# Linear attention with a GEGLU block on one core: the order of the k-v products and of v, and the size of the last q groups

One core of one Trainium2 chip. The metric is the device time of one execution in microseconds, taken on the slowest core, here the only one. All executions quoted are fast, at a granted TensorE clock of 1.0 (0.999 in some).

## The reference

A layer norm, an attention whose features are softmaxes of a small per-head product, a second layer norm and a GEGLU block, over 2048 rows of 640 columns, in bfloat16:

```python
pq = einsum("bhsd,hdf->bhsf", q, w_phi);  pk = einsum("bhsd,hdf->bhsf", k, w_phi)
phi_q = concat([softmax(pq), softmax(-pq)], -1);  phi_k = the same of pk
kv = einsum("bhsf,bhsd->bhfd", phi_k, v);  z = phi_k summed over s
o = einsum("bhqf,bhfd->bhqd", phi_q, kv) / (einsum("bhqf,bhf->bhq", phi_q, z)[..., None] + 1e-6)
h  = x + o.reshape(B, S, D) @ wo
h2 = h + (gelu(LN(h) @ w_gate) * (LN(h) @ w_up)) @ w_down
```

## The kernel before

The 2048 rows are 16 tiles of 128. For each tile t a loop issues the k projection (with `w_phi` folded in) and its two exponentials, then the v projection of tile t+4, the layer norm of tile t+6, whose transpose goes through a DMA to `LN1T`, and the normalising factors of k. At odd tiles the k-v products of two earlier tiles are added to an accumulator in PSUM. The order is set by hand, and in the traces PE's products come in the order in which they are written. In the profiles `pk` and `pv` are the k and v products of a tile, `wa` the folding of `w_phi` into the weights of q, `kvp` the k-v products, `pq` the products of a group of q and `Eq` their exponentials, `ab` and `po` the attention and output products of a tile, `gu` the gate and up products, `g` the gelu and `GT` its product with up. Shortened, with cuts marked:

```python
QG = ((0, 1), (2, 3), ..., (13, 14), (15,), (16, 17), (18, 19))   # groups of chunks of q

def kv_tile(t):                       # 20 products of 64 x 84, into one PSUM tile
    ...
for t in range(NT):
    ...
    k_tile(t)                         # 10 products, then two exponentials on ScalarE
    if t in FQ: fold(WqT, Wq2, ...)   # tiles 4 to 8: 6 small products ("wa")
    ...
    if t + 4 < NT: v_mm(t + 4)        # 10 products; they need tile t+4 of LN1T
    if t > 0 and t + 6 < NT: ln_ap(t + 6, on_act=True)   # layer norm, then the DMA transpose
    if t + 4 < NT: v_ev(t + 4)        # ScalarE copies v out of PSUM
    ...
    k_norm(t)
    if t % 2 == 1 and t >= 5:         # k-v products behind v
        kv_tile(t - 5)
        kv_tile(t - 4)

def q_mm(j):                          # one PSUM tile of two banks for a group
    pqs[j] = gtile("pq")
    for i, bc in enumerate(QG[j]): ...  # 5 products of 512 columns for each chunk
def q_exp(j, signs=(0, 1)):           # exp(x) and exp(-x) of the whole group
    for s in signs:
        nc.scalar.activation(Eq[j][:, :, s, :], pqs[j][:, 0:len(QG[j])], ACTF.Exp, scale=(1.0, -1.0)[s])
```

The loop has three PSUM tiles for k, v and the folded weights. Behind the loop the attention of the first tiles and the rest of q are interleaved on four PSUM tiles, and the gate and up products (`gu`) follow. A chunk of q is 128 features over 512 rows. Between the last exponential and the first gelu ScalarE loads another table (1.28 us in the trace).

The softmax here doesn't subtract the row's maximum and nothing guards it: scores larger than these inputs give would overflow.

## Time and profile before

| | before |
|---|---|
| time, median of 3 (later 6) | 280.98 (280.89) us |
| span of the profiled execution | 278.9 us |
| TensorE (PE) busy | 272.0 us |
| PE waits that the change is about | v of tile 9, v of tile 11, third gate/up group |

The change goes for three waits of PE. They are read in the timeline from start to start, since the ends that the profile gives for PE are modelled and overlap the next start. The groups of ScalarE by form, with the count, busy time and mean ns of one, price the exponentials of q:

```profile
L352 ACT ACTIVATE Eq<-pq 128x1024 bf16<-128x1024 f32 x18 | 17.5, 1026 | 3.7 <-PE pq L347 3.7
L352 ACT ACTIVATE Eq<-pq 128x512 bf16<-128x512 f32 x4 | 2.2, 612 | 0.0
```

One instruction over two chunks (1026 ns) is cheaper than two over one each (2 x 612 ns). The other lines of this profile stand in the prediction; its list of PE's waits shows three of six rows, and the three left out (0.2 to 0.4 us) lie in the first 16 us.

### The profile page before, as it was taken

The page shows a single profiled execution, that of the slowest core. Times are in us where ns is not written, and L with a number is a line of the kernel's source. Part 1 is how long each engine was busy: PE and PEld are TensorE (multiplying, and loading weights), DVE is VectorE, ACT ScalarE, POOL GpSimd, SP SyncE. Part 2 cuts the span into 40 slices and gives each one's busy share as a digit, 9 for nine tenths or more (in the row PEclk, how much of TensorE's full clock was granted, in tenths as well). Part 3 has the DMA queues.
Part 4 walks back from the last instruction along what each step waited for, and adds up shares of the span by engine and source line. Part 5 has one row for each costly group of instructions (what it writes and reads, how often), then busy time and mean ns, then how long its engine had stood idle before and what let it go on. Part 6 is the DMA issues. An engine that isn't in the chain of part 4 may idle for free.

```text
span 278.9 us, 5775 instructions
## 1 busy us (share of the span) xinstructions
PE 272.0 (98%) x2322; PEld 171.8 (62%) x2337; DVE 165.0 (59%) x289; ACT 142.3 (51%) x235; POOL 95.8 (34%) x211
## 2 busy tenths in 40 slices
PE   7999999999999999999999999999999999999995
PEld 2677677764655788788864555675455567444574
DVE  5799997789396586576324848322667532333222
ACT  4669988768596847355524354413446340222200
POOL 3448997685202216455401243300135230000000
DMA  7995222893440021314120113221041413000011
GB/s 208 271 244 83 51 51 47 175 396 138 144 143 0 2 48 26 71 46 98 27 71 2 40 21 61 44 75 47 2 47 24 74 24 94 26 1 0 0 49 47
DMA packets 40635, 21.05 MB, mean 75 GB/s; under 512 B 33440, under 2 KB 38816, under 8 KB 40608
## 3 DMA queue, kind: packets, MB, share of 16 engines
q1 hardware_dynamic: 40608, 20.68, 29.9%
q8 instruction: 18, 0.29, 0.5%
q14 instruction: 9, 0.07, 0.1%
HBM read 10.18 MB, written 2.62 MB: 46 GB/s over the span
## 4 chain that ended last, share of the span: by engine, by line
PE 89%; DMA 3%; ACT 2%; DVE 2%; issue 1%; POOL 1%; SPq 0%
PE gu L588 37%; PE pd L609 19%; PE pq L347 8%; PE po L543 8%; PE pk L260 7%; PE pv L260 5%; PE ab L483 3%; PE kvp L325 2%; DMA LN1T<-ln 2%; DMA x_sb<-in_A_x_dram 1%; ACT Eq L352 1%; DVE stats L108 1%; ACT sq L357 1%; PE wa L224 1%; PE tp L145 1%
## 5 line engine op out<-in xcount | busy, mean ns | idle before, releaser
L594 DVE TENSOR_TENSOR GT<-gu,g 128x512 bf16<-128x512 f32 (+1 forms) x60 | 34.4, 580 | 55.2 <-ACT g L591 55.1
L591 ACT ACTIVATE g<-gu 128x512 bf16<-128x512 f32 (+1 forms) x60 | 30.7, 512 | 69.1 <-PE gu L588 68.2
L588 PE MATMUL gu<-LN2T,Wg 128*128 128x512 bf16 (+1 forms) x289 | 61.3, 335 | 1.0 <-DVE GT L594 0.4
L588 PE MATMUL gu<-LN2T,Wu 128*128 128x512 bf16 (+1 forms) x300 | 61.8, 336 | 0.0
L609 PE MATMUL pd<-Wd,GT 128*128 128x320 bf16 (+2 forms) x396 | 53.8, 295 | 0.0
L609 PEld LDWEIGHTS <-GT 128*128 128x128 bf16 x396 | 38.0, 98 | 15.3 <-DVE GT L594 0.9
L588 PEld LDWEIGHTS <-Wu 128*128 128x128 bf16 x300 | 29.3, 98 | 22.6
L588 PEld LDWEIGHTS <-Wg 128*128 128x128 bf16 x300 | 28.3, 98 | 21.3 <-issue 0.5
L260 PEld LDWEIGHTS <-LN1T 128*128 128x128 bf16 x290 | 27.6, 98 | 11.6 <-DMA LN1T<-ln 0.7
L307 POOL TENSOR_TENSOR vt<-vS,rs 128x672 bf16<-128x672 bf16 x22 | 29.7, 1371 | 8.7 <-DVE rs L303 7.0
L614 DVE TENSOR_TENSOR y<-pd,x_sb 128x640 bf16<-128x640 f32 (+3 forms) x18 | 13.5, 750 | 30.2 <-PE pd L609 30.2
L491 ACT COPY AB<-ab 128x704 f32<-128x704 f32 x28 | 19.6, 748 | 19.8 <-PE ab L483 19.6
L299 DVE TENSOR_REDUCE sk<-E 128x64 f32<-128x1280 bf16 x16 | 23.1, 1446 | 3.7 <-ACT E L292 3.7
L292 ACT ACTIVATE E<-pk 128x640 bf16<-128x640 f32 x32 | 20.9, 707 | 7.9 <-PE pk L260 7.7
L524 DVE TENSOR_TENSOR tt<-AB,w 128x1280 bf16<-128x1280 f32 x16 | 23.8, 1486 | 1.1 <-POOL w L517 0.9
L543 PE MATMUL po<-Wo,oT 128*128 128x320 bf16 x160 | 24.4, 299 | 0.0
L260 PE MATMUL pk<-Wk,LN1T 128*128 128x320 bf16 x160 | 24.2, 299 | 0.0
L347 PE MATMUL pq<-LN1T,Wq 128*128 128x512 bf16 x96 | 22.7, 379 | 0.2
L352 ACT ACTIVATE Eq<-pq 128x1024 bf16<-128x1024 f32 (+1 forms) x22 | 19.4, 951 | 3.7 <-PE pq L347 3.7
L260 PE MATMUL pv<-Wv,LN1T 128*128 128x320 bf16 x130 | 20.0, 299 | 0.5 <-DMA LN1T<-ln 0.5
L543 PEld LDWEIGHTS <-oT 128*128 128x128 bf16 x160 | 15.5, 98 | 7.3 <-DMA oT<-o 0.5
L132 ACT ACTIVATE ln<-x_sb,v,rstd 128x640 bf16<-128x640 bf16 x14 | 12.9, 919 | 11.3 <-POOL v L571 11.1
(89 smaller groups left out, 262.9 us busy)
## 6 DMA issues: line engine op xcount, KB each, us to landing
out_dram<-y SPq DMA_DIRECT2D x15, 160.0 KB, 1.8
Wg<-in_B_w_gate_dram SPq DMA_DIRECT2D x1, 1920.0 KB, 8.5
Wu<-in_B_w_up_dram SPq DMA_DIRECT2D x1, 1920.0 KB, 15.0
Wd<-in_B_w_down_dram SPq DMA_DIRECT2D x1, 1920.0 KB, 8.0
x_sb<-in_A_x_dram SPq DMA_DIRECT2D x2, 640.0 KB, 5.5
Wo<-in_A_wo_dram SPq DMA_DIRECT2D x1, 800.0 KB, 9.5
x_sb<-in_A_x_dram SPq DMA_DIRECT2D x4, 160.0 KB, 3.1
Wv<-in_A_wqkv_dram SPq DMA_DIRECT2D x2, 320.0 KB, 4.4
```

The source lines that it names most:

```text
L260: nc.tensor.matmul(ps[:, u, 0:HD], lhsT=lnT(t, c), rhs=W[:, c, u * HD:(u + 1) * HD], start=(c == 0), stop=(c == NC - 1))
L292: nc.scalar.activation(Ek[t][:, s, :].rearrange("p (u f) -> p u f", u=2), pk[:, :, 0:HD], ACTF.Exp, scale=(1.0 if s == 0 else -1.0))
L299: nc.vector.reduce_sum(sk, Ek[t].rearrange("p s (h f) -> p (s h) f", f=Dh), axis=AX.X)
L307: eng.tensor_tensor(vt[:, s], vS[t % 8], rs[:, s * H:(s + 1) * H, None].to_broadcast([P, H, VC]), ALU.mult)
L347: nc.tensor.matmul(pqs[j][:, i, :], lhsT=Wq2[:, kc, c * P:(c + 1) * P], rhs=LN1T[b][:, kc, :], start=(kc == 0), stop=(kc == NC - 1))
L352: nc.scalar.activation(Eq[j][:, :, s, :], pqs[j][:, 0:len(QG[j])], ACTF.Exp, scale=(1.0, -1.0)[s])
L524: nc.vector.tensor_tensor(tt.rearrange("p s (h f) -> p s h f", f=Dh), num, w[:, :, :, None].to_broadcast([P, 2, H, Dh]), ALU.mult)
L543: nc.tensor.matmul(po[:, u, 0:HD], lhsT=st[t][:, c, :], rhs=Wo[:, c, u * HD:(u + 1) * HD], start=(c == 0), stop=(c == NC - 1))
L588: nc.tensor.matmul(gu[:, i, 0:n], lhsT=W[:, c, f * P:(f + 1) * P], rhs=LN2T[b][:, c, a0:a1], start=(c == 0), stop=(c == NC - 1))
L591: nc.scalar.activation(g[:, 0:n], gu[:, 0, 0:n], ACTF.Gelu_apprx_tanh)
L594: nc.vector.tensor_tensor(st[b, "g", f][:, a0:a1], gu[:, 1, 0:n], g[:, 0:n], ALU.mult)
L609: nc.tensor.matmul(pd[:, u, n0:n1], lhsT=st[b, "g", f][:, tl * P:(tl + 1) * P], rhs=Wd[:, f, u * HD + n0:u * HD + n1], start=(f == 0), sto ...
```

## The change

Two independent parts. The k-v products of a pair of tiles go ahead of the next v, so that PE has work while v waits. And the last four chunks of q, two groups of two before, become four groups with their own PSUM tiles and exponentials, so that ScalarE is done sooner after the last product of q and can change its table.

```diff
-    QG = (..., (15,), (16, 17), (18, 19))
+    QG = (..., (15,), (16,), (17,), (18,), (19,))
...
+        if t % 2 == 1 and t >= 5:
+            kv_tile(t - 5)
+            kv_tile(t - 4)
         if t + 4 < NT:
             v_mm(t + 4)
...
         k_norm(t)
-        if t % 2 == 1 and t >= 5:
-            kv_tile(t - 5)
-            kv_tile(t - 4)
...
     attn_c(1)
-    q_mm(q + 5)
-    q_exp(q + 5)
+    for j in (q + 5, q + 6):
+        q_mm(j)
+        q_exp(j)
     attn_ln(0, True); attn_d(1, False); attn_e(0, True, True)   # (three lines, unchanged)
-    q_mm(q + 6)
-    q_exp(q + 6)
+    for j in (q + 7, q + 8):
+        q_mm(j)
+        q_exp(j)
```

More of the change, by code (lines that the diff above doesn't have):

```diff
@@ L50 @@
     FQ = (4, 5, 6, 7, 8)
-    QG = ((0, 1), (2, 3), (4, 5), (6,), (7, 8), (9, 10), (11, 12), (13, 14), (15,), (16, 17), (18, 19))
+    QG = ((0, 1), (2, 3), (4, 5), (6,), (7, 8), (9, 10), (11, 12), (13, 14), (15,), (16,), (17,), (18,), (19,))
     QT = (15, 15, 15, 15)
@@ L682 @@
     attn_a(2, 2)
-    assert q + 7 == len(Eq)
+    assert q + 9 == len(Eq)
     def attn_at(t, i, offs):
```

## The prediction

> **What bounds the kernel now.** I read the page first. TensorE (PE) is busy 272.0 us of a 278.9 us span and carries 89% of the chain that ended last.
>
> ```profile
> span 278.9 us, 5775 instructions
> PE 272.0 (98%) x2322; PEld 171.8 (62%) x2337; DVE 165.0 (59%) x289; ACT 142.3 (51%) x235; POOL 95.8 (34%) x211
> ```
>
> So whatever is to be won lies in at most 278.9 - 272.0 = 6.9 us of PE idle time. Of that, 1.24 us stands before the first matmul and most of the rest in the first 16 us and in the store at the end, which the change does not touch. Next I read the waits of PE alone. Its columns are engine, line, what was waited for, us in total, times and the longest.
>
> ```profile
> PE wu L206 <- DVE zero L191: 1.2, 1, 1.2
> PE pv L260 <- DMA LN1T<-ln: 0.5, 1, 0.5
> PE gu L588 <- DVE GT L594: 0.4, 1, 0.4
> ```
>
> The second and third rows are the two places where the change acts: one wait of a v product for its transposed input, and one wait of the first gate/up products for a PSUM buffer. To price them I read the timeline of PE around each (start, duration, line, operation, count, idle time before it).
>
> ```profile
> 30.46 1.52 PE L260 MATMUL pk<-Wk,LN1T 128*128 128x320 bf16 x10
> 31.82 0.48 PE L224 MATMUL wa<-BD,WqT 128*128 128x140 bf16 x6
> 32.77 1.53 PE L260 MATMUL pv<-Wv,LN1T 128*128 128x320 bf16 x10 [0.48 <-DMA LN1T<-ln]
> 34.23 0.95 PE L325 MATMUL kvp<-vt,E 128*64 128x84 bf16 x40
> 35.12 1.53 PE L260 MATMUL pk<-Wk,LN1T 128*128 128x320 bf16 x10
> ...
> 39.52 0.48 PE L224 MATMUL wa<-BD,WqT 128*128 128x140 bf16 x6
> 40.02 1.52 PE L260 MATMUL pv<-Wv,LN1T 128*128 128x320 bf16 x10
> 41.47 0.96 PE L325 MATMUL kvp<-vt,E 128*64 128x84 bf16 x40
> 42.36 0.85 PE L260 MATMUL pk<-Wk,LN1T 128*128 128x320 bf16 x5
> ```
>
> Durations overlap, because ends are modelled; I therefore work with the distance between starts. Six wa products take 29.10 - 28.79 = 0.31 us where nothing holds them up, so PE was free at 31.82 + 0.31 = 32.13 and really lost 32.77 - 32.13 = 0.64 us, not 0.48. By the same measure pv at 40.02 came 40.02 - 39.83 = 0.19 us late. No DMA is named there. In the order of instructions this pv reuses the PSUM buffer that the previous v leaves, and ScalarE (ACT) copied that one out from 39.27 to 39.97.
>
> The second place, ACT, PE and VectorE (DVE) side by side:
>
> ```profile
> 91.24 1.94 ACT L352 ACTIVATE Eq<-pq 128x1024 bf16<-128x1024 f32 x2 [0.50 <-PE pq L347]
> 93.20 1.28 ACT L591 ACT_TABLE_LOAD   x1
> 94.49 0.38 ACT L591 ACTIVATE g<-gu 128x256 bf16<-128x256 f32 x1
> ...
> 94.91 0.42 DVE L594 TENSOR_TENSOR GT<-gu,g 128x256 bf16<-128x256 f32 x1 [1.20 <-ACT g L591]
> ...
> 94.30 0.71 PE L588 MATMUL gu<-LN2T,Wu 128*128 128x256 bf16 x5
> 95.39 0.71 PE L588 MATMUL gu<-LN2T,Wg 128*128 128x256 bf16 x5 [0.37 <-DVE GT L594]
> ```
>
> It is one chain: last exponentials of q, table load, first gelu, its product, and only then is the buffer of the first gate/up group free for the third group. Five products of 256 columns take 0.55 us from start to start (94.30 - 93.76), so PE was free at 94.85 and lost 0.54 us.
>
> **What the Trainium skill says.** "TensorE: Matmul & The Clock Gate", section Back-to-back issue gap, gives N/2.4 + 2.5 ns for a warm matmul, 136 ns at 320 columns; here ten take 1.36 us (30.46 to 31.82), so PE runs at that rate and moving products makes none cheaper. The same page, Step-by-step: what each phase is for, says that matmuls stay in program order and only weight loads are pulled ahead; the trace agrees, as ready k-v products stood behind the waiting v at 32.77. "ScalarE: Activation LUTs", section What ACT_TABLE_LOAD costs, gives 186 ns + 0.833 ns per element for an activation with immediate scale and bias, 93 ns of overlap, and about 1283 ns for a load. The trace has 612 and 1026 ns for 512 and 1024 columns and 1283 ns for the load, which agrees; the page's extra 1380 ns of drain is not seen, the gelu starts 0.01 us after the load. "Perfetto Trace Analysis", section Optimizing Scalar/DVE Operations, advises breaking up instructions of an unsaturated engine that causes bubbles on others; the second half of the change does that.
>
> **The change, part 1: k-v products ahead of v.** The count of PE instructions stays 2322. At tiles 5, 7, 9 and 11 forty k-v products (0.89 us, 34.23 to 35.12) change places with the ten v products. Are they ready? The first pair needs products that POOL and DVE had finished by 29.2 us, so yes, by 3 us. At tile 5 PE then runs: wa ends 32.13, about 0.10 us for the switch to 64-column products (v before k-v takes 1.46 instead of 1.36 us today, so this is paid either way), k-v to 33.12, v to 34.48. Its input landed by about 32.7, so it no longer waits. The next k starts at 34.48 instead of 35.12: **0.64 us**. At tile 7 everything is 0.64 earlier. The v-copy on ACT that held the buffer follows its own v and ends near 39.33; PE reaches the k-v products at 39.2 and v only at 40.18. So the 0.19 is hidden too: k at 41.54 instead of 42.36, **0.82 us** in all. At tiles 9 and 11 v starts without a delay today (46.76, 53.19), so the swap brings nothing. Its cost is that each v is copied out 0.89 us later relative to the k before it; ACT has 1.24, 0.78 and 0.88 us of idle time before the exponentials of the following k, and that is the gap it eats.
>
> **Part 2: single groups.** Four activations of 1024 columns become eight of 512. ACT pays 4 x (0.48 + 0.61) - 2 x (0.92 + 1.02) = 0.48 us more (spacing and last duration of each form), inside 1.94 and 0.50 us that it idles there. The path gets shorter: chunk 18 is done before chunk 19 ends, so from 91.24 only two short exponentials are left, 0.48 + 0.61 = 1.09 us instead of 1.94. Table load from 92.35, gelu at 93.64, its product about 94.05 to 94.47, which is before PE asks at 94.85. The wait goes: **0.54 us**.
>
> **Sum**: 0.82 + 0.54 = 1.36 us of span. I take off 0.1 for small new waits: 281.0 - 1.3 = **279.7 us**.
>
> **Rivals.** (1) The input wait moves on instead of going. One transpose took 4.3 us to land where most take 2.6; v of tile 10 would now want its input at 36.16 instead of 36.80, and if that transfer (issued 31.71) takes 4.3 it lands at 36.0. For it: the margin is 0.15 us. Against: at 36.80 no wait is seen. It would leave about 0.2 + 0.54: 280.2 us. (2) PSUM takes the place. A single group occupies a whole one of four buffers and half of it is empty, so the second half of the attention product of tile 2 now waits for chunk 18's exponentials, done at about 91.24, and is wanted at 91.42. If ACT runs 0.3 us late there, PE waits and part 2 brings 0.2 or less: 280.1 us. (3) The gain of part 2 is given back at 101.48, where the output product of tile 2 takes its weights just as a DMA transpose lands (the trace shows 0.16 us of waiting). PE comes there 0.54 us earlier; only if DVE also gets earlier is nothing lost. For DVE: its work for that tile stands behind the first two gelu products, which move 0.4 to 0.9 us forward, so the transpose should land at about 100.6, before 100.97. If not, 280.2 us. (4) Nothing at all, if the 4.3 us landing is an accident of the profiled execution and the untimed ones never wait: then only part 2 counts, 280.4 us.
>
> **Range and chances.** All rivals lie between 279.7 and 281, and nothing in the change can touch the 98% that PE works. The three runs before differ by 1.4 us, more than the gain, so I give 278.8 to 280.9. Two per cent is 5.6 us, nearly the whole idle time of PE, so faster by that much gets 0.02. Slower would take a new wait of 5 us or a slow execution: 0.01.
>
> **What would show it.** Right: PE's waits no longer name LN1T for pv and GT for gu; the k after the first k-v products starts near 34.5 and the one after the second near 41.5; the table load starts near 91.5 (93.20 less 0.82 from part 1 and 0.85 from part 2); PE busy time stays 272. Wrong: a new wait of pv for LN1T or ACT between 36 and 42, a wait of ab for Eq near 90.6, or a wait for oT near 100; or a span that falls by less than 0.8 us.

## The result, and the profile after

| | before | after |
|---|---|---|
| time, median of 6 (range) | 280.89 us (280.68 to 282.08) | 279.53 us (279.02 to 280.40) |
| ratio, 95% interval | | 0.9947 (0.9922 to 0.9972) |
| span of the profiled execution | 278.9 us | 278.0 us |
| PE busy | 272.0 us | 272.2 us |

A ratio is the mean time of one kernel's fast runs over that of the other's of the same rounds, so it is not quite the ratio of the medians. The interval leaves 1 out. The medians differ by 1.36 us, which the prediction had as its sum before it took 0.1 off. The profiled spans differ by only 0.9 us, and that needs an explanation. The waits of PE after:

```profile
PE wu L206 <- DVE zero L191: 1.2, 1, 1.2
PE pv L260 <- DMA LN1T<-ln: 0.3, 1, 0.3
PE wa L224 <- DVE Wk L235: 0.2, 1, 0.2
PE pv L276 <- DVE LN1T L146: 0.2, 1, 0.2
```

The wait for GT is gone. A wait of pv for LN1T is still in the list, but the timeline of PE shows that it is a different one:

```profile
23.83 1.53 PE L260 MATMUL pv<-Wv,LN1T 128*128 128x320 bf16 x10 [0.31 <-DMA LN1T<-ln]
...
30.95 1.52 PE L260 MATMUL pk<-Wk,LN1T 128*128 128x320 bf16 x10
32.31 0.48 PE L224 MATMUL wa<-BD,WqT 128*128 128x140 bf16 x6
32.72 0.95 PE L325 MATMUL kvp<-vt,E 128*64 128x84 bf16 x40
33.60 1.53 PE L260 MATMUL pv<-Wv,LN1T 128*128 128x320 bf16 x10
34.97 1.52 PE L260 MATMUL pk<-Wk,LN1T 128*128 128x320 bf16 x10
...
39.36 0.48 PE L224 MATMUL wa<-BD,WqT 128*128 128x140 bf16 x6
39.77 0.96 PE L325 MATMUL kvp<-vt,E 128*64 128x84 bf16 x40
40.66 1.53 PE L260 MATMUL pv<-Wv,LN1T 128*128 128x320 bf16 x10
42.03 1.52 PE L260 MATMUL pk<-Wk,LN1T 128*128 128x320 bf16 x10
```

The first row is v of tile 6, which started at 23.35 in before and now waited, long before anything that the change moves; PE is 0.49 us late from there (k of tile 5 at 30.95 instead of 30.46). The k after the first k-v products then stands at 34.97 instead of 35.12: against k of tile 5 it is 0.64 us earlier. The next one, at 42.03 instead of 42.36, is 0.82 us earlier by the same measure. ScalarE and PE around the change of table:

```profile
87.38 2.16 ACT L352 ACTIVATE Eq<-pq 128x512 bf16<-128x512 f32 x4 [0.86 <-PE pq L347]
89.81 2.17 ACT L352 ACTIVATE Eq<-pq 128x512 bf16<-128x512 f32 x4 [0.27 <-PE pq L347]
92.00 1.28 ACT L591 ACT_TABLE_LOAD   x1
93.29 0.38 ACT L591 ACTIVATE g<-gu 128x256 bf16<-128x256 f32 x1
```

```profile
93.96 0.71 PE L588 MATMUL gu<-LN2T,Wu 128*128 128x256 bf16 x5
94.50 0.71 PE L588 MATMUL gu<-LN2T,Wg 128*128 128x256 bf16 x5
```

The table load came 1.31 us after the start of the last transposes (90.69), before 2.16 us (91.04 to 93.20): 0.85 us earlier. The third gate/up group follows the second without a gap, 0.54 us after 93.96, where before there were 1.09.

To compare runs in spite of accidents in the start-up I use three stretches of PE's timeline, from start to start: from k of tile 0 to k of tile 5 (start-up), from there to k of tile 12 (where part 1 acts), and from there to the third gate/up group (where part 2 acts). In us:

| | start-up | part 1's stretch | part 2's stretch |
|---|---|---|---|
| before | 14.36 | 25.07 | 39.86 |
| after | 14.85 | 24.25 | 39.30 |
| change | +0.49 | -0.82 | -0.56 |

The three add up to -0.89, the 0.9 us between the spans. What lies outside them is the same in these two (16.10 us ahead of k of tile 0; 183.51 and 183.50 from the third gate/up group to the end), but over all fourteen profiles it varies: 15.89 to 16.61 and 183.40 to 184.05 us. The start-up's 0.49 is no effect of the change, as the runs below show.

### The profile page after: what moved, and what is told of

Read it like the earlier page. It is cut to its first block, busy times and chain, and to the rows that moved or that the text cites. A ratio compares the mean times of both kernels' runs of the same rounds, so it can differ in the third digit from the quotient of the medians.

```text
span 278.0 us, 5780 instructions
## 1 busy us (share of the span) xinstructions
PE 272.2 (98%) x2322; PEld 172.5 (62%) x2337; DVE 165.2 (59%) x289; ACT 142.9 (51%) x239; POOL 96.1 (35%) x211
## 4 chain that ended last, share of the span: by engine, by line
PE 93%; DVE 3%; DMA 1%; POOL 1%; issue 1%; POOLq 0%
PE gu L588 38%; PE pd L609 19%; PE pq L347 8%; PE po L543 8%; PE pk L260 6%; PE pv L260 5%; PE ab L483 3%; PE kvp L325 2%; PE wu L206 2%; DMA LN1T<-ln 1%; PE pv L276 1%; DVE stats L108 1%; PE tp L145 1%; DVE Wk L235 1%; PE wa L224 1%
```

## The experiments

Each edit is against the kernel before unless it says otherwise. All results were correct. All had five rounds beside the kernel before on the same chip. Their stretches, and the landing times (issue to landing in us) of the DMA transposes of tiles 6 and 9, are in one table:

| run | ratio (95%) | start-up | part 1's | part 2's | tile 6 | tile 9 |
|---|---|---|---|---|---|---|
| before (profile) | | 14.36 | 25.07 | 39.86 | 3.5 | 4.3 |
| after (profile) | | 14.85 | 24.25 | 39.30 | 4.1 | 4.2 |
| e1 k-v ahead only | 0.9960 (0.9933 to 0.9987) | 14.36 | 24.25 | 39.84 | 2.6 | 4.2 |
| e2 single groups only | 0.9972 (0.9945 to 1.0000) | 15.11 | 24.93 | 39.31 | 4.4 | 4.2 |
| e3 last pair single | 0.9987 (0.9957 to 1.0018) | 14.37 | 25.05 | 39.64 | 3.6 | 4.3 |
| e4 halves in one group | 1.0005 (0.9972 to 1.0039) | 14.37 | 25.01 | 39.99 | 3.6 | 4.3 |
| e5 after again | 0.9951 (0.9925 to 0.9978) | 14.36 | 24.26 | 39.30 | 2.6 | 4.2 |
| e6 k-v ahead at 5 only | 0.9972 (0.9950 to 0.9995) | 15.33 | 24.42 | 39.86 | 4.6 | 4.2 |
| e7 small DMA | 1.0013 (0.9987 to 1.0040) | 15.60 | 24.91 | 39.85 | 4.8 | 4.2 |
| e8 fewer switches | 0.9939 (0.9915 to 0.9963) | 15.70 | 24.03 | 39.06 | 5.0 | 4.3 |
| e9 k-v ahead at 9, 11 only | 0.9989 (0.9966 to 1.0012) | 14.42 | 24.99 | 39.84 | 3.7 | 4.2 |
| e10 first pair single | 0.9988 (0.9965 to 1.0010) | 14.59 | 24.92 | 39.85 | 3.8 | 4.2 |
| e11 fewer switches, late x | 0.9928 (0.9903 to 0.9953) | 14.52 | 24.02 | 39.07 | 2.6 | 2.6 |
| e12 late x only | 0.9981 (0.9967 to 0.9994) | 14.55 | 24.43 | 39.86 | 2.6 | 2.6 |

The intervals are some 0.25% (0.7 us) to each side, wider than most of the effects. The stretches, in contrast, repeat to 0.02 us where the kernels have the same order and the same waits (24.25, 24.25, 24.26; 39.30, 39.30, 39.31). So a verdict on 0.2 us below rests on the stretches; the ratios only don't contradict them.

**e1, part 1 alone.**

```diff
+        if t % 2 == 1 and t >= 5: kv_tile(t - 5); kv_tile(t - 4)     # ahead of v_mm(t + 4), and not behind k_norm
```

> Only the first half: k-v products ahead of v, q groups as before. My theory (they fill the wait of v for its input at tile 5 and the wait for a buffer at tile 7): 0.82 us less than before, ratio about 0.997; in the profile the k after the first k-v products starts 2.84 us after the wa products before it are done (34.97 - 32.13 in before plus the wait hidden), the pv with LN1T wait at tile 5 gone, and the wait of 0.4 for GT at the third gate/up group still there. Rival (the q groups bring the whole gain, the k-v order only moves a wait): no more than 0.2 us.

Part 1's stretch is 24.25 instead of 25.07, part 2's is unchanged, and the wait for GT is still in the list of PE's waits:

```profile
PE gu L591 <- DVE GT L597: 0.4, 1, 0.4
```

So the order brings 0.82 us by itself; the rival (0.2 us at most) falls. The ratio, 0.9960, is 1.1 us; its interval holds the 0.82. The profiled span is only 0.4 us shorter (278.5), because in this execution k of tile 0 started 0.19 us later than in before and the stretch behind the third group was 0.25 us longer. One figure of my expectation was wrong: the 2.84 us took one end from before and the other from after. From the end of the wa products (32.01 + 0.31) to the next k (34.68) it is 2.36 us.

**e2, part 2 alone.**

```diff
-(16, 17), (18, 19)
+(16,), (17,), (18,), (19,)          # and the calls that go with it; k-v products behind v
```

> Only the second half: last four chunks of q as single groups, k-v products behind v. My theory: 0.54 us less than before, ratio about 0.998; table load 0.85 us earlier relative to the last q product than before, no wait for GT at the third gate/up group, wait of pv for LN1T near 32.8 still there. Rival (PSUM or the output transpose takes it back): 0.2 us or less, with a new wait of ab for Eq or of po for oT.

Part 2's stretch is 39.31 instead of 39.86, that is 0.55 us, and no new wait of `ab` or `po` shows. Of v of tile 9 the wait is still there, beside the accidental one of tile 6 at 24.28:

```profile
24.28 1.53 PE L260 MATMUL pv<-Wv,LN1T 128*128 128x320 bf16 x10 [0.58 <-DMA LN1T<-ln]
33.57 1.53 PE L260 MATMUL pv<-Wv,LN1T 128*128 128x320 bf16 x10 [0.34 <-DMA LN1T<-ln]
```

Between the two waits a trade is seen: where PE is late already, the second wait is shorter (0.34 instead of 0.48). The parts add up: 0.82 + 0.55 against 0.82 + 0.56 together.

**e3, only the last pair single.**

```diff
-(16, 17), (18, 19)
+(16, 17), (18,), (19,)
```

> Only the last pair of chunks of q (18 and 19) as two groups; 16 and 17 stay one group; k-v order as before. My theory (the path is the exponentials between the last q product and the table load): the same 0.54 us as all four single. Rival (the gain needs the earlier exponentials of 16 and 17 too): clearly less than 0.54, third gate/up group still waits.

My expectation fell: part 2's stretch is 39.64, which is 0.22 us of the 0.55. There is no wait for GT any more, but another has come. ScalarE's timeline and PE's:

```profile
88.64 3.90 ACT L352 ACTIVATE Eq<-pq 128x1024 bf16<-128x1024 f32 x6 [1.94 <-PE pq L347]
92.56 1.28 ACT L591 ACT_TABLE_LOAD   x1
```

```profile
91.25 0.91 PE L483 MATMUL ab<-KV,Eq 64*128 64x88 bf16 x20
92.09 0.72 PE L588 MATMUL gu<-LN2T,Wg 128*128 128x256 bf16 x5
```

The two long exponentials of chunks 16 and 17 start only when both are multiplied, and with four more behind them ScalarE works 3.90 us without a pause. Chunk 18's come too late for the attention product of tile 2, which wants their PSUM tile: its first product starts at 91.25 and the other 19 at 91.61, 0.05 us after the second of these exponentials ended (90.94 + 0.62), so the 20 take 0.91 instead of 0.57 us. The copies of `ab` on VectorE then end at 93.87, and the second gate/up group starts at 93.92, 0.12 us late. The chain of work in this profile names both releasers, and with the first delay of some 0.2 us they make up the missing 0.33 us. That is rival 2 of the prediction, a wait for PSUM in the place of the one removed. In the whole change it doesn't appear, because chunks 16 and 17 are done earlier.

**e10, only the first pair single.**

```diff
-(16, 17), (18, 19)
+(16,), (17,), (18, 19)
```

> Chunks 16 and 17 of q as single groups, 18 and 19 still one group; k-v order as before. The other half of the single groups. Run e3 had half of the gain in its profile, because the 1024-column exponentials of 16 and 17 ran until 90.5 and held up those of chunk 18. Theory: without the split of 18 and 19 the last 1.94 us stay, so the table load stays in its place and the gain is 0.0 us, the wait for GT stays at 0.4. Rival (each pair brings its half): 0.2 to 0.3 us.

39.85 instead of 39.86: nothing, and the wait for GT stays at 0.4. So the first split earns nothing by itself, the last one 0.22, both 0.55. The split of 18 and 19 shortens the path and that of 16 and 17 frees it from ScalarE's backlog.

**e4, small exponentials in the same group.**

```diff
-    q_exp(q + 6)
+    for i in range(2):                     # chunk by chunk
+        for s in range(2):
+            nc.scalar.activation(Eq[j][:, i, s, :], pqs[j][:, i], ACTF.Exp, scale=(1.0, -1.0)[s])   # j = q + 6
```

> Groups as before, but the last group of two chunks gets four exponentials of 512 columns instead of two of 1024; the program lets all of them wait for the last of its ten products. My theory (what counts is that chunk 18 can be done while the products of 19 run, not the size of the instruction): four times 0.48 plus 0.13 is 2.05 instead of 1.94 us, so the table load comes 0.11 us later and the time is the same as before or 0.1 us more. Rival (smaller exponentials by themselves shorten the path): 0.4 to 0.5 us less.

As my theory had it: the four take 2.06 us and all start after the last product of chunk 19, and the stretch is 39.99, 0.13 us longer than before.

```profile
91.42 2.06 ACT L357 ACTIVATE Eq<-pq 128x512 bf16<-128x512 f32 x4 [0.50 <-PE pq L347]
93.50 1.28 ACT L596 ACT_TABLE_LOAD   x1
```

Smaller instructions alone cost; what pays is that a chunk with its own tile can be exponentiated while the next is multiplied.

**e5, the changed kernel again.** No edit against it.

> The changed kernel once more, beside the others of this call on one chip. Both theories: 1.36 us less than before, ratio 0.995; in its profile the distance from the last start-up product to the third gate/up group is 1.36 us shorter than in before wherever v of tile 6 doesn't wait.

24.26 and 39.30, and a start-up of 14.36 as in before: this time tile 6's transpose landed in 2.6 us. The span is 277.6 us, 1.3 below before's 278.9. This shows that the 0.49 us in the first profile of the changed kernel was an accident of that execution.

**e6, ahead at tile 5 only.**

```diff
+        if t == 5: kv_tile(0); kv_tile(1)        # ahead of v; at the other odd tiles behind it, as before
```

> k-v products ahead of v at tile 5 alone, at tiles 7, 9 and 11 behind it as before; q groups as before. My theory: this one place hides 0.64 us (the wait for tile 9's transpose, which landed after 4.2 to 4.3 us in all six profiles so far); ratio about 0.9977; v of tile 11 still comes about 0.1 to 0.7 us late, because it now meets the copy of v or its own input earlier. Rival (the wait moves on to the next v): 0.2 us or less, with a new wait near 36 to 40 us.

The stretch is 24.42: 0.65 us from this place alone. No new wait follows at tile 10, where its transpose lands in 2.6 us. The remaining 0.17 (24.42 to 24.25) is what the swap at tile 7 brings, as those at 9 and 11 bring nothing (e9).

**e9, ahead at tiles 9 and 11 only.** The same edit with `t in (9, 11)`.

> Control: k-v products ahead of v only at tiles 9 and 11, where v starts without delay in the kernel before; behind v at 5 and 7; q groups as before. My theory (the move pays only where v waits): same time as before, 0.0 us; the distance between the k of tile 9 and the k of tile 12 is 10.13 us as in before (45.40 to 55.53). Rival (k-v products next to k are cheaper in themselves, or the order helps ACT): 0.1 us or more per moved pair.

From k of tile 9 (45.34) to k of tile 12 (55.48) it is 10.14 us, as in before: the swap itself earns nothing where v doesn't wait. The stretch is 0.08 shorter than before's, but that lies at tile 5: k of tile 5 came later in this run and v of tile 9 waited 0.38 instead of 0.48.

**e7, a small load behind tile 9's transpose.**

```diff
+        if t == 3: nc.sync.dma_start(scr, A_wo[0:16, 0:16])    # behind ln_ap(9)
```

> The kernel before with one 512-byte load into an unused tile issued behind tile 9's transpose. Theory A (that transpose lands after 4.3 us because of its place in the queue, and lands when something follows it): it lands in 2.6 us, v of tile 9 doesn't wait, and 0.64 us are gained without moving any product; this would confirm the wait as the source of that part of the gain. Theory B (the slow landing has nothing to do with what follows): it still lands after about 4.3 us, PE waits as before, same time as before.

It still landed after 4.2 us and v of tile 9 still waited (0.31). Theory A falls: what follows in the queue is not the reason.

**e12, the last load of x later.**

```diff
-    nc.sync.dma_start(x_sb[3], x_v[:, 12:16, :])      # 640 KB, ahead of the transpose of tile 6
+        if t == 1: nc.sync.dma_start(x_sb[3], x_v[:, 12:16, :])     # behind the transpose of tile 7
```

> The kernel before with nothing changed but the last 640 KB load of x, issued behind tile 7's transpose instead of ahead of tile 6's. In e11, which has the same order of loads, tile 6's and tile 9's transposes both landed in 2.6 us; in all ten other profiles tile 9's took 4.2 to 4.3. If the order of loads is the cause: both land in 2.6 us here too, v of tile 9 comes without a wait although the k-v products still stand behind it, and the time is 0.6 us or more below before (ratio 0.998 or less); then the wait, and not the place of the products, is shown to be what part 1 removed. If e11 was chance: tile 9 lands after about 4.2 us, v of tile 9 waits 0.3 to 0.5 us, same time as before.

Tile 9's transpose landed in 2.6 us, as in e11 and in none of the twelve profiles with the old order of loads. PE's timeline has the k-v products still behind v, and v follows the wa products at 0.32 us, without a wait:

```profile
28.70 0.48 PE L223 MATMUL wa<-BD,WqT 128*128 128x140 bf16 x6
29.21 1.53 PE L259 MATMUL pv<-Wv,LN1T 128*128 128x320 bf16 x10
...
31.93 0.48 PE L223 MATMUL wa<-BD,WqT 128*128 128x140 bf16 x6
32.25 1.52 PE L259 MATMUL pv<-Wv,LN1T 128*128 128x320 bf16 x10
33.70 0.96 PE L324 MATMUL kvp<-vt,E 128*64 128x84 bf16 x40
...
38.99 0.48 PE L223 MATMUL wa<-BD,WqT 128*128 128x140 bf16 x6
39.49 1.52 PE L259 MATMUL pv<-Wv,LN1T 128*128 128x320 bf16 x10
```

The stretch is 24.43, which is 0.64 us less without any product moved, where e6 had 0.65. So it is the wait for this one input that part 1 removed at tile 5. At tile 11 (38.99 to 39.49) v is still 0.19 late, as in before. Its input is not the reason, as that transpose landed near 37.5 (34.86 + 2.6); it fits a wait for the copy that frees its PSUM tile, which ends at 39.44. The late load also has a price: it now runs beside the transpose of tile 8, which landed in 3.6 us (3.5 in e11) instead of the 2.6 of the twelve other profiles, that is at 29.2. The first rows above show v of tile 8 start there, 0.20 us late. The waits view doesn't name it; it is why the start-up is 14.55 and not 14.36. It takes back 0.19 of the 0.64, and the time fell by 0.5 us (0.9981), not by the 0.6 or more that I expected. Why tile 9's transpose (and tile 12's, at 4.1 to 4.4 us in all fourteen profiles) lands late, and why the order of loads four transposes earlier changes it, stays open.

**e8, fewer switches**, against the changed kernel.

```diff
-        if t % 2 == 1 and t >= 5: kv_tile(t - 5); kv_tile(t - 4)
+        if t in (5, 7): kv_tile(t - 5); kv_tile(t - 4)
+        if t == 11: kv_tile of 4, 5, 6, 7
...
-    for t in range(12, NT): kv_tile(t)
+    for t in range(8, NT): kv_tile(t)
```

> The changed kernel with the k-v products gathered: pairs ahead of v at tiles 5 and 7, four tiles at once at tile 11, tiles 8 to 15 behind q. Each switch from full-width to 64-column products costs PE about 0.10 us, and this has two fewer: 0.2 us less than the changed kernel (ratio to before about 0.994), below what five rounds resolve but visible as starts in the profile. Rival (ACT or the buffers of the k-v operands make PE wait when a pair of k-v products is missing between two k): 0 to 0.5 us more than the changed kernel, with a wait of pk or pv for ACT near 47 to 55 us.

Part 1's stretch is 0.22 shorter than the changed kernel's (24.03 for 24.25) and part 2's 0.24 (39.06 for 39.30): 0.46 us, more than twice what I expected. A pair by itself costs 0.98 us (0.89 and 0.09 more in the k ahead of it); a second pair in the same run only 0.76, as the two take 1.65 us together:

```profile
51.87 1.52 PE L260 MATMUL pk<-Wk,LN1T 128*128 128x320 bf16 x10
53.32 1.72 PE L325 MATMUL kvp<-vt,E 128*64 128x84 bf16 x80
54.97 1.53 PE L260 MATMUL pv<-Wv,LN1T 128*128 128x320 bf16 x10
```

I had counted the switch into the 64-column products and forgotten the one out of them. In the timed runs the gain over the changed kernel doesn't show against the start-up: medians 279.46 (e8) and 279.40 (e5).

**e11, e8 with the load of e12.**

> A version meant to beat both: as e8, and the last 640 KB load of x issued behind tile 7's transpose instead of ahead of tile 6's. In the profiles so far tile 6's transpose took 2.6 to 5.0 us to land, and v of tile 6 waited for it up to 1.2 us. If it is that load that stands in its way: it lands in 2.6 us, no wait of v of tile 6, and the time is 0.3 to 0.8 us below e8 (ratio to before about 0.992), with less spread. If it is the transposed load of the q weights: no change. Danger: the load meets tile 8's transpose, and v of tile 8 or the statistics of tile 12 wait.

The best version: median 279.07 us, ratio 0.9928, all six runs between 278.78 and 279.85, and no wait for LN1T among PE's waits, though v of tile 8 comes 0.15 us late as in e12. It beats the kernel before. That it beats the changed kernel (0.9947 and 0.9951) is likely from its profile, whose span is 277.1 us against 278.0 and 277.6, and not shown by the intervals, which overlap. Tile 6's transpose landed in 2.6 us here and in e12, but so it did by chance in e1 and e5, so two profiles are thin evidence that the late load cures tile 6. The danger that I named came true in part: the lateness went to tile 8.

## Why the prediction was right

The time lay 0.17 us below the predicted 279.7, well within the range. That it came so close is partly luck, as the interval of the ratio allows a gain of 0.8 to 2.2 us; each step can be checked by its own number.

- **0.64 us at tile 5**: measured 0.64 in after and 0.65 in e6. e12 removes the same wait by another way and gains the same 0.64.
- **0.19 us at tile 7**: measured 0.17 to 0.18. That v waits there for a PSUM tile was read from the order of instructions and from a copy on ScalarE that ends 0.05 us before v starts. The runs agree (in e12, with the input early, the delay stays), but none removed that copy alone, so the copy as the cause is argued and not shown.
- **Nothing at tiles 9 and 11**: e9 shows nothing.
- **0.54 us from the single groups**: measured 0.55 (e2). The chain as told, exponentials, table, gelu, product, buffer, moved by 0.85 us, and PE no longer waits for it.
- **Reading from start to start**: the waits view gave 0.48 and 0.37 for the two waits, 0.85 us in sum. The prediction took 0.64 and 0.54 from the starts and added 0.19 that no wait names; the stretches confirm these.
- **The rivals**: (1) the input wait did not move to tile 10, whose transpose landed in 2.6 us. (2) The wait for PSUM is real but only where one pair is split (e3); the prediction's margin of 0.18 us held in the full change. (3) The output product of tile 2 lost nothing: its transpose was issued at 97.66 instead of 98.86 and landed in 2.6 us, near 100.3, some 0.3 us ahead of the product at 100.57, where the prediction expected 0.4. (4) The 4.3 us landing is no accident but came in all twelve profiles with that order of loads.
- **Where it was off**: the table load was forecast near 91.5 and came at 92.00, and the profiled span fell by 0.9 and not 1.36. The missing term is the start-up: the prediction took everything ahead of tile 5 as fixed, and in the profiles it varies from 14.36 to 15.70 us with the landing of tile 6's transpose: up to 3.6 us it costs nothing, at 4.1 us the start-up is 14.85 and at 5.0 us 15.70 (e11 and e12 lose theirs at tile 8). Nothing in the change acts there, but that it averages out over six runs is not shown, and it is as large as each half of the gain. The 0.1 us taken off for small new waits was not needed: in e5 the two stretches are 0.81 and 0.56 us shorter.
- **Two readings to correct**: that moving products makes none cheaper holds for the pairs moved here, but e8 gathers pairs and saves 0.46 us, and PE's busy time falls from 272.1 (e5) to 271.0. And N/2.4 + 2.5 ns, which the prediction quotes for a warm matmul from "TensorE: Matmul & The Clock Gate", section Back-to-back issue gap, is there the gap of a single isolated one; for streams of large products the page expects less, 131 ns at 512 columns. In this case streams do run at the formula's rate, 136 ns at 320 columns (30.46 to 31.82, ten) and 216 at 512 (88.88 to 91.04, ten), so the step rests on the trace.

## What to carry to other kernels

On an engine that is full nearly all the time, price a wait from start to start in the timeline and look also for delays that no wait names; then put ready work ahead of the instruction that waits, only at the places where it waits. Here splitting an instruction shortened the path only where its parts got their own buffers, so that they could start earlier (e4), and where the engine was not still busy with the long ones ahead of them (e3). Where effects are a few tenths of a per cent, compare stretches of the timeline that start behind the noisy part, beside the timed runs.

## What the Trainium skill lacked or had wrong

- "TensorEngine Tiling (Array Packing)", section Key Properties, says that a change of tiling mode drains TensorE and gives no figure. Here a pair of k-v products (128*64 in the profile) between full-width ones (128*128) costs 0.98 us and in a longer run 0.76, so a change there and back costs some 0.22 us (e8); that a drain is what costs it is not shown.
- "ScalarE: Activation LUTs", section What ACT_TABLE_LOAD costs, adds about 1380 ns of drain to a load of about 1283 ns. Here the load took 1283 ns, started 0.02 us after the last exponential and the first gelu started 0.01 us after it (before and after).
- "Perfetto Trace Analysis", section Optimizing Scalar/DVE Operations, advises breaking up instructions of an engine that causes bubbles elsewhere. It lacks the condition that e4 shows: split inside one buffer, the path became 0.13 us longer; split with a buffer for each part, 0.55 us shorter.
- No page gives the spread of the landing of a DMA transpose. Here 160 KB took 2.6 us in most cases, 2.6 to 5.0 for tile 6 beside a 640 KB load, 3.5 and 3.6 for tile 8 when that load was moved beside it (e11, e12), and 4.2 to 4.3 or 2.6 for tile 9, depending on the order of earlier loads (e12).
